# A one-core S4 and PEER mix: the first matmul work is taken from the experts' scores, a row sum is done twice, and a weights' buffer is claimed later

## The chip, the cores and the metric

The kernel runs on one core of a Trainium2 chip. That core has five engines with an instruction stream each: TensorE (PE, matmuls), VectorE (DVE), ScalarE (ACT), GpSimd (POOL) and SyncE (SP), which here issues nearly all DMA transfers. The metric is the device time of one execution in microseconds, and the figure for a kernel is the median of three runs.

## The reference

For 2048 tokens of 576 numbers the program computes two branches and mixes them by a gate:

```
x = A_u                                       # (1, 2048, 576)
g = sigmoid((x * gate_w).sum(-1))
a = S4 convolution of x along the tokens (kernel K from 128 complex poles
    for each of 576 channels, by FFT) + x * Dskip
b: q = x @ w_q                                # 32 heads, two halves of 128
   s1 = q1 . k1, s2 = q2 . k2                 # 64 keys each
   top 2 of s1 and top 2 of s2, 4 sums, top 2 of these -> experts e, softmax g2
   act = gelu(x . u[e])                       # 4096 experts, u, v: (4096, 576)
   b = sum over heads and picks of g2 * act * v[e]
out = g * a + (1 - g) * b
```

## The kernel before

The kernel doesn't gather expert rows. It computes `x . u` for all 4096 experts, places the chosen weights in a dense array of 2048 tokens by 4096 experts, and multiplies that with `v`. Nearly all of TensorE's time is in three products: the scores `s` (tokens by keys, where the keys have been folded into `w_q`), the activations `a` (experts by tokens), and the output `o`. Each is done with operands split into a high and a low fp16 part, three matmuls for one, so each operand is first scaled by a power of two that is found from sums of squares.

Names. `xT` is the tokens, transposed; `xb[tb]` is a block of 512 tokens, scaled and split (`xb[:, 0:4]` high parts, `4:8` low parts, `8` the last 64 of the 576 rows with both). `xs` and `xr` are its raw data in fp32 (512 rows and the last 64). `uhl[c]` with `wrem` is a chunk of 512 experts of `u`, scaled and split in the same way, from raw `us` and `ur`. `whl[c]` with `wrem` is a chunk of four heads of folded weights, built in two halves from raw `wq` (`w_half`): squares on ACT (`wj`), a row sum on PE (`wn`), a fold with the keys on PE (`wb`, 72 small matmuls), and the scaled split on ACT and DVE (`w_tail`). A group `s(c,t)` is 14 matmuls for 128 tokens, followed on DVE by 8 MAX8 and 8 FIND_INDEX8; a group `a(c,tb,j)` is 14 matmuls for 128 experts and 512 tokens, followed by one scaled copy `go` and a store to `g_d`.

What sets the order. The kernel is recorded by cooperating generators under a planner in the kernel's own Python: `clock` is planned PE time, `Engine` objects estimate when each engine is free and each tile is ready, `spawn`, `ready` and `need` suspend a generator until the planned time of its inputs, a PSUM bank or a buffer. The recorded order is final: at run time each engine takes its instructions strictly in that order, and SP its DMA issues. Counted places stand for buffers (`quota`): `slot` 9 large SBUF buffers, `raw` one place (later two) for a raw chunk of `wq` or `us` in work, `sc` four PSUM banks for `s` and `a`.

The head of the program before: SP issues the keys `kt`, the first tokens, the two halves of the first weights, then the first `u`. PE sums the squares of the first tokens (`x`, 5 matmuls), folds both halves of the weights, and then begins with `s(0,0)`. The main loop then takes groups from the lists `groups` (scores) and `acts` (activations) as their inputs come ready. At a change of weights chunk, `w_next` may claim `raw` for the first half of the next chunk once 5 groups of the current chunk are left; the place is given back when that half has been folded, and the fold needs `w_build(c)`, which waits for the last group of the chunk before.

Alongside, from about 100 us to 600 us, the generators of the S4 branch run: `k_front` and `k_gen` (GpSimd, DVE and ACT, with PE's `kP` and `kb`), and `u_stage1`. After that come the transforms, the placing of the picks (`S`), and the output `o`.

Of the kernel before, what the change touches and what calls it, by code (L numbers as in the profile page):

```python
# [13 lines left out]
F16 = mybir.dt.float16  # L14
# [102 lines left out]
class Engine:  # L117


    def __init__(self, eng, ready, clock, key, cost):  # L120
        self.eng, self.ready, self.clock, self.key, self.cost = eng, ready, clock, key, cost
        self.free = 0.0

    def __getattr__(self, op):
        f = getattr(self.eng, op)

        def call(*a, **k):
            out = k.get("out", a[0] if a else None)
            aps = [x for x in (*a, *k.values()) if x is not out and hasattr(x, "tensor")]
            start = max(self.free, self.clock[0], *(self.ready.get(self.key(x), 0.0) for x in aps))  # L130
            self.free = start + self.cost(op, out, a, k)
            self.ready[self.key(out)] = max(self.free + 0.28, self.ready.get(self.key(out), 0.0))
# [5 lines left out]
def body(ctx: ExitStack, tc: tile.TileContext, xT, au, par, logdt, dskip, gatew, wq, kT, uT, vv,  # L138
# [283 lines left out]

    def x_load(tb):
# [3 lines left out]
        dma(a, xT[0:512, c].rearrange("(k p) n -> p k n", p=128))  # L427
        dma(r[0:64], xT[512:576, c])
        dma(r[64:128], xT[512:576, c])
        return a, r  # L430
# [14 lines left out]

    def x_build(tb):
        while tb and tb - 1 not in scaled:
            yield 0.3
        if tb:
# [3 lines left out]
        while tb and 0 not in uhl:  # L453
            yield 0.3
        b = slot([9, 512], F16, f"xb{tb}")
        sq = b[:, 0:5].bitcast(BF16)
        yield from ready(a, r)
        if tb:
            S.activation(sq[:, 0:4, :], a, AF.Square)
        else:  # L460
            S.activation(sq[:, 0:2, :], a[:, 0:2], AF.Square)
            V.tensor_mul(sq[:, 2:4, :], a[:, 2:4], a[:, 2:4])
        S.activation(sq[:, 4, :], r, AF.Square)
        yield from ready(b)
        yield from need("kb")
        p = bank("kb", f"x{tb}")
        for k in range(5):
            mm(p, onesb, sq[:, k, :], k == 0, k == 4)
        yield from ready(p)
        V.tensor_reduce(out=nx[:, tb:tb + 1], in_=p, axis=AX, op=OP.max)  # L470
        free("kb", nx)
        s, i = root_scale(nx[:, tb:tb + 1], 1.02)
        V.tensor_copy(i_x[:, tb:tb + 1], i)
        yield from ready(s)
        for o, i in [(b[:, k], a[:, k, :]) for k in range(4)] + [(b[:, 8], r)]:
            if tb == 0 or S.free > V.free + 2.0:
                V.tensor_scalar(o, i, s, None, op0=OP.mult)
            else:
                S.activation(o, i, AF.Copy, scale=s)
        scaled.append(tb)  # L480
        for k in range(4):
            yield from ready(b)
            V.scalar_tensor_tensor(b[:, 4 + k], a[:, k, :], s, b[:, k], op0=OP.mult, op1=OP.subtract)
# [9 lines left out]
    whl, wl, sk, halves, scaled, squared = {}, {}, [], {}, [], []  # L493
# [23 lines left out]

    def w_half(c, h, w):
        fl = lambda x: x.rearrange("p a b -> p (a b)")
        yield from ready(w)  # L520
        pbs = []
# [1162 lines left out]
```

## Time and profile before

| | us |
|---|---|
| median of 3 runs | 1469.38 |
| lowest and highest | 1467.86, 1471.87 |
| the profiled execution | 1466.58 |
| its span, first to last instruction | 1464.7 |
| PE busy | 1431.2 (98%) |
| DVE busy | 1248.5 (85%) |
| ACT busy | 790.6 (54%) |
| POOL busy | 532.0 (36%) |

The profiled execution is 2.8 us faster than the median of the runs. All waits and durations below are from it. Its span leaves out 1.9 us that lie before the first and after the last instruction.

The page's line numbers are of the kernel before. All work on DVE, ACT and POOL has L133 (the `Engine` helper), all matmuls L213 and all DMA issues L204, so rows are told apart by the names of their tiles. A matmul's duration in a row includes its fill; the rate of a run of matmuls is read from the starts.

### The profile page before, as it was taken

To read this page: it belongs to the slowest core of one execution; us is meant where nothing else is said; L and a number is where in the kernel's file an instruction comes from. 1 tells how busy PE (TensorE), PEld (TensorE's weight loads), DVE (VectorE), ACT (ScalarE), POOL (GpSimd) and SP (SyncE) were. 2 spreads that over 40 slices of the span, in tenths; PEclk is the share of its full clock that TensorE was granted. 3 is DMA by queue.
4 is the path that set the end of the run, shared out by engine and by line. 5 is a ranking of instruction groups with operands and counts; after the bars stand their busy time and mean duration, and the time that the engine had idled before them with its cause. 6 is when DMAs were issued, how large, how long until landed. Compare 5 with 4: busy or idle time off the path is not lost.

```text
span 1464.7 us, 36789 instructions
## 1 busy us (share of the span) xinstructions
PE 1431.2 (98%) x14025; PEld 858.4 (59%) x14028; DVE 1248.5 (85%) x4589; ACT 790.6 (54%) x1315; POOL 532.0 (36%) x511
## 2 busy tenths in 40 slices
PE   5999999999999999999999999998999999999999
PEld 2445454554544544555555444455787787788787
DVE  6989989989999699959899898579998998898860
ACT  5647767698697787434656544576424224223310
POOL 0443545556745645201246799622100110110100
PEclk8999999999999999999999999999999999999999
DMA  9235433372434534384768666677533432442400
GB/s 319 81 93 162 128 94 118 111 213 89 147 104 133 160 107 135 109 263 138 254 211 290 232 200 206 221 239 221 157 111 116 133 125 85 138 147 68 156 10 17
DMA packets 139185, 221.21 MB, mean 151 GB/s; under 512 B 11648, under 2 KB 82688, under 8 KB 132608
## 3 DMA queue, kind: packets, MB, share of 16 engines
q1 hardware_dynamic: 138912, 218.78, 46.5%
q8 instruction: 110, 1.80, 0.5%
q14 instruction: 67, 0.55, 0.1%
q10 hardware_dynamic: 96, 0.07, 0.0%
HBM read 147.51 MB, written 71.30 MB: 149 GB/s over the span
## 4 chain that ended last, share of the span: by engine, by line
PE 84%; DVE 10%; DMA 3%; ACT 1%; issue 1%; SPq 1%; POOL 1%; DVEq 0%; ACTq 0%; POOLq 0%
PE o L213 24%; PE a L213 23%; PE s L213 22%; PE S L213 4%; PE wb L213 2%; PE kb L213 2%; DVE i L133 2%; PE pr L213 2%; DVE m L133 1%; PE u L213 1%; PE y L213 1%; PE kP L213 1%; DVE e L133 1%; PE pv L213 1%; DVE uh L133 1%
## 5 line engine op out<-in xcount | busy, mean ns | idle before, releaser
L213 PE MATMUL o<-vhl,wh 128*128 128x288 f16 x3072 | 387.0, 286 | 0.0
L213 PE MATMUL s<-whl,xb 128*128 128x512 f16 x1536 | 369.5, 382 | 5.0 <-DVE whl L133 4.2
L213 PE MATMUL a<-xb,uhl 128*128 128x512 f16 x1536 | 361.1, 379 | 0.4 <-DVE ko L133 0.4
L213 PEld LDWEIGHTS <-wh 128*128 128x128 f16 x3072 | 296.0, 98 | 76.3 <-issue 3.7
L213 PEld LDWEIGHTS <-xb 128*128 128x128 f16 x1792 | 171.8, 98 | 213.1 <-issue 27.1
L213 PEld LDWEIGHTS <-uhl 128*128 128x128 f16 x1536 | 148.2, 98 | 175.7 <-issue 2.8
L133 DVE FIND_INDEX8 i<-m,s 128x8 uint32<-128x64 f32 x1024 | 206.5, 222 | 0.0
L133 ACT ACTIVATE wh<-gl,s_wg 128x1024 f16<-128x1024 f32 x64 | 68.9, 1137 | 200.3 <-DVE gl L133 200.3
L133 DVE MAX8 m<-s 128x8 f32<-128x64 f32 x1024 | 146.4, 215 | 28.1 <-PE s L213 27.8
L133 POOL TENSOR_TENSOR CS<-CS,ex 128x512 f32<-128x512 f32 x72 | 100.2, 1423 | 139.0 <-DVE ex L133 120.0
L133 POOL TENSOR_TENSOR ya<-ya,db 128x576 f32<-128x576 f32 x16 | 32.0, 2012 | 305.2 <-DMA ya<-in_au_dram 143.6
L133 ACT ACTIVATE go<-a,i_a 128x512 f32<-128x512 f32 x95 | 64.2, 686 | 82.5 <-PE a L213 54.7
L133 POOL TENSOR_TENSOR e<-aN,rt 128x512 f32<-128x512 f32 x72 | 87.5, 1234 | 50.9 <-PE kb L213 47.6
L133 DVE SCALAR_TENSOR_TENSOR wh<-gl,s_wg,wh 128x1024 f16<-128x1024 f32 x64 | 92.4, 1474 | 11.3 <-ACT wh L133 11.3
L133 DVE TENSOR_TENSOR gl<-S,gl 128x256 f32<-128x256 f32 x256 | 90.0, 415 | 7.3 <-PE S L213 7.3
L133 DVE TENSOR_TENSOR Bg<-Be,vals 128x1024 f16<-128x1024 f16 x128 | 90.6, 749 | 2.2
L133 ACT ACTIVATE gl<-gl 128x1024 f32<-128x1024 f32 x64 | 63.5, 1045 | 34.8 <-DMA gl<-g_d 34.8
L133 DVE TENSOR_TENSOR A<-iota_a,vals 128x2048 f16<-128x2048 f16 x64 | 80.5, 1258 | 0.0
L213 PE MATMUL S<-Bg,A 128*128 128x64 f16 x2048 | 73.0, 193 | 5.1 <-DVE Bg L133 4.2
L213 PEld LDWEIGHTS <-A 128*128 128x128 f16 x2048 | 70.6, 97 | 11.2 <-DVE Bg L133 4.1
L213 PE MATMUL s<-wrem,xb 128*128 128x512 f16 x256 | 76.2, 379 | 0.0
L213 PE MATMUL a<-xb,wrem 128*128 128x512 f16 x256 | 76.2, 379 | 0.0
(203 smaller groups left out, 2205.7 us busy)
## 6 DMA issues: line engine op xcount, KB each, us to landing
g_d<-go SPq DMA_DIRECT2D x128, 256.0 KB, 2.7
gl<-g_d SPq DMA_DIRECT2D x32, 1024.0 KB, 5.4
wq<-in_wq_dram SPq DMA_DIRECT2D x16, 1152.0 KB, 6.3
us<-in_au_dram SPq DMA_DIRECT2D x64, 144.0 KB, 3.0
su_d<-us SPq DMA_DIRECT2D x32, 288.0 KB, 2.6
sk_d<-k1o SPq DMA_DIRECT2D x32, 288.0 KB, 2.8
vn<-in_vv_dram SPq DMA_DIRECT2D x32, 288.0 KB, 3.7
ui<-su_d SPq DMA_DIRECT2D x16, 576.0 KB, 4.0
```

Of the source, the lines that this page charges most:

```text
L133: return f(*a, **k)
L213: T.matmul(o, l, r, start=start, stop=stop)
```

## The change

Three things are changed, and the planner's order follows from them in the whole program.

1. The head. SP issues the first tokens (the remainder first, then two halves) and the first `u` in the same way, then the keys, the second block of tokens, the weights and the constants. `x_first` and `scale_first` scale the first tokens by the whole block's sum of squares (taken by ACT's accumulator, summed over partitions by PE in three one-column matmuls) instead of the largest row sum. The first 56 matmuls of PE's main work are `a(0,0,0..3)`, recorded piece by piece: for each part of the tokens and of `u`, four matmuls as soon as it is planned to be there. The folds of the first weights (`fold_first`), their squares and `kn` come later, after the second block of tokens has its scale.
2. `x_norm(0)` computes the row sums of the first tokens twice: 8 matmuls whose result is overwritten while the scale of `u` is not there, and then the 5 that count.
3. `w_next` claims `raw` when 2 groups of the current chunk are left, not 5; the second half of a chunk (`second`) goes ahead of a chunk of `u` that waits for the same place.

Beside these, `Engine.at` lets the planner count a result as ready 0.16 us earlier on the engine that made it, and `x_build` waits for each scaled part by itself.

```diff
+    def halves_load(a, src, c):
+
+        columns.add(a.tensor.name)
+        for m in (0, 2):
+            dma(a[:, m:m + 2], src[128 * m:128 * m + 256, c].rearrange("(k p) n -> p k n", p=128))
...
+    def x_norm(tb, sq):
+
+        yield from need("kb")
+        p = bank("kb", f"x{tb}")
+        if tb == 0:
+            for k in range(8):
+                mm(p, onesb, sq[:, k % 4, :], True, True)
+            while not marks["s"]:
+                yield 0.1
+        for k in range(5):
+            mm(p, onesb, sq[:, k, :], k == 0, k == 4)
+        normed.append(tb)
+        yield from ready(p)
+        while tb == 0 and 1 not in scaled:
+            yield 0.3
+        V.tensor_reduce(out=nx[:, tb:tb + 1], in_=p, axis=AX, op=OP.max)
+        free("kb", nx)
+
+    def x_first():
+
+        a, r = xl.pop(0)
+        b = slot([9, 512], F16, "xb0")
+        first_u[1] = b
+        ahead.append(slot([9, 512], F16, "xb1"))
+        sq = ahead[0][:, 0:5].bitcast(BF16)
+        s, i = yield from scale_first(a, r, sq)
+        spawn(x_norm(0, sq))
+        V.tensor_copy(i_x[:, 0:1], i)
+        for k in range(5):
+            while k == 2 and not marks["s"]:
+                yield 0.1
+            o, lo, src = (b[:, k], b[:, 4 + k], a[:, k, :]) if k < 4 else (b[:, 8], b[64:128, 8], r)
+            p = slice(0, 128) if k < 4 else slice(64, 128)
+            V.tensor_scalar(o, src, s, None, op0=OP.mult)
+            V.scalar_tensor_tensor(lo, src[p], s[p], o[p], op0=OP.mult, op1=OP.subtract)
+            marks["x"].append(V.free + 0.28)
+        scaled.append(0)
+        free("slot", b)
+        xb.append(b)
+
+    def scale_first(a, r, sq, keep=None):
+
+        acc = [newcol() for _ in range(3)]
+        yield from ready(r)
+        S.activation(sq[:, 4], r, AF.Square, accum_out=sc[:, acc[0]])
+        for n, m in enumerate((0, 2)):
+            yield from ready(a[:, m:m + 2])
+            S.activation(sq[:, m:m + 2], a[:, m:m + 2], AF.Square, accum_out=sc[:, acc[n + 1]])
+        yield from ready(sq)
+        yield from need("kb")
+        p = bank("kb", "sq")
+        for n in range(3):
+            mm(p[:, 0:1], onesb, short(acc[n].start, 1), n == 0, n == 2, 0.05)
+        yield from ready(p)
+        out = root_scale(p[:, 0:1], 1.02)
+        if keep is not None:
+            V.tensor_copy(keep, p[:, 0:1])
+        free("kb", out[0])
+        return out
...
+    def fold_first(h, w, pbs):
+        while len(folded) < h or 1 not in scaled:
+            yield 0.2
+        out = []
+        yield from need("kb", 3 + h)
+        yield from w_fold(0, h, w, out, ("kb",) * 3)
+        pbs.extend(out)
+        folded.append(h)
...
+        if c == 0:
+            spawn(fold_first(h, w, pbs))
+        while 1 not in scaled:
+            yield 0.2
...
     def w_next(c, h):
-        while sdone[0] < c - (kdone[0] == NCK) and 8 * NT - len(groups) < NT * c - 5:
+        while sdone[0] < c - (kdone[0] == NCK) and 8 * NT - len(groups) < NT * c - 2:
             yield 0.3
         yield from need("raw")
         take("raw", "raw")
+        if h:
+            second.pop()
...
+        if c == 0:
+            first_u[0] = hl
+            s, i = yield from scale_first(a, r, sq, nu[:, 0:1])
+            marks["s"].append(1)
...
+        if c == 0:
+            for k in range(4):
+                S.activation(hl[:, 0, k, :], a[:, k, :], AF.Copy, scale=s)
+                marks["h"].append(S.free + 0.28)
+            S.activation(rem[:, 0, :], r, AF.Copy, scale=s)
+            marks["h"].append(S.free + 0.28)
         for k in range(4):
-            yield from split(hl[:, 0, k, :], hl[:, 1, k, :], a[:, k, :], s)
-        S.activation(rem[:, 0, :], r, AF.Copy, scale=s)
+            if c:
+                yield from split(hl[:, 0, k, :], hl[:, 1, k, :], a[:, k, :], s)
+                continue
+            while 0 not in scaled:
+                yield 0.1
+            rdy[key(hl)] = marks["h"][k]
+            V.scalar_tensor_tensor(hl[:, 1, k, :], a[:, k, :], s, hl[:, 0, k, :], op0=OP.mult, op1=OP.subtract)
+            marks["u"].append(V.free + 0.28)
...
+    xl = {0: x_load(0)}
+    take("raw", "raw")
+    xl["u"] = u_load(0)
     dma(kt, kT)
-    xl = {0: x_load(0)}
+    xl[1] = x_load(1)
     w_load(0, 0)
     w_load(0, 1)
+    dma(cst, cst_d[:, :KT])
...
+    spawn(x_first())
+    spawn(u_build(0))
+    spawn(w_build(0), 4)
+    spawn(w_half(0, 0, wl[0, 0]), 4)
+    spawn(w_half(0, 1, wl[0, 1]), 4)
+    spawn(k_split(), 4)
+    for tb in range(1, 4):
+        spawn(x_build(tb), 5 * tb)
     spawn(k_params(), 30)
...
+    until(lambda: marks["x"] and marks["h"], 0.1)
+    first = [bank("sc", f"a0_0_{j}") for j in range(4)]
+
+    def landed(kind, k):
+        until(lambda: len(marks[kind]) > k, 0.1)
+        idle(max(0.0, marks[kind][k] - clock[0]))
+
+    for w, n in ((0, 9), (1, 5)):
+        for xk in [x for k in range(4) for x in (k, 4 + k)[:2 - w]] + [8]:
+            k = 4 if xk == 8 else xk % 4
+            landed("x", k)
+            landed("hu"[w], k)
+            for j in range(4):
+                cs = slice(128 * j, 128 * j + 128)
+                mm(first[j], wrems[0][:, w, cs] if k == 4 else first_u[0][:, w, k, cs], first_u[1][:, xk, :],
+                   w == 0 and xk == 0, w == 1 and k == 4)
+            pump()
+    del acts[0:4]
+    if 0 in i_u:
+        V.tensor_scalar(i_a[:, 0, 0:1], i_x[:, 0:1], i_u[0], None, op0=OP.mult)
+    for j in range(4):
+        spawn(act_post(0, 0, j, first[j]))
```

Line numbers in the order below are of each kernel: L133 and L204 before are L140 and L211 now. SP at the head of the program, before:

```order
L204 DMA kt_113<-in_kT_dram 128x128
L204 DMA xs0_119<-in_xT_dram 128x4x512
L204 DMA xr0_120<-in_xT_dram 64x512 x2
L204 DMA wq0_0_124<-in_wq_dram 128x2304
L204 DMA wq0_1_126<-in_wq_dram 128x2304
L204 DMA us0_142<-in_uT_dram 128x4x512
L204 DMA ur0_143<-in_uT_dram 64x512 x2
L204 DMA cst_70<-in_cst_dram 128x576
L204 DMA xs1_210<-in_xT_dram 128x4x512
```

and now:

```order
L211 DMA xr0_119<-in_xT_dram 64x512 x2
L211 DMA xs0_118<-in_xT_dram 128x2x512 x2
L211 DMA ur0_125<-in_uT_dram 64x512 x2
L211 DMA us0_124<-in_uT_dram 128x2x512 x2
L211 DMA kt_113<-in_kT_dram 128x128
L211 DMA xs1_131<-in_xT_dram 128x4x512
L211 DMA xr1_132<-in_xT_dram 64x512 x2
L211 DMA wq0_0_136<-in_wq_dram 128x2304
L211 DMA wq0_1_138<-in_wq_dram 128x2304
L211 DMA cst_70<-in_cst_dram 128x576
```

The first `u` has moved from behind both halves of the weights to a place behind the first tokens, and both are issued in two halves; the keys, which were first, stand behind them.

ScalarE at the head (`xb` and `uhl` with `sc` are squares into the place of the later split, `uhl` with `sci` are the scaled high parts, `vals` is the squares of the keys), before:

```order
L133 ACTIVATE vals_80<-kt_113 128x128
L133 ACTIVATE xb0_136<-xs0_119 128x1024
L133 ACTIVATE xb0_136<-xr0_120 128x512
L133 ACTIVATE wj0_0_163,sc_75<-wq0_0_124 128x1152 x2
L133 ACTIVATE wj0_1_223,sc_75<-wq0_1_126 128x1152 x2
L133 ACTIVATE whl0_135<-wb0_0_2_167,sci_76 128x2x256
L133 ACTIVATE wrem2_116<-wb0_0_4_168,sci_76 64x128 x4
L133 ACTIVATE uhl0_282,sc_75<-us0_142 128x2048
L133 ACTIVATE uhl0_282,sc_75<-ur0_143 128x512
L133 ACTIVATE whl0_135<-wb0_1_0_226,sci_76 128x2x256
L133 ACTIVATE whl0_135<-wb0_1_2_227,sci_76 128x2x256
L133 ACTIVATE wrem2_116<-wb0_1_4_228,sci_76 64x128 x4
```

and now:

```order
L140 ACTIVATE xb1_149,sc_75<-xr0_119 128x512
L140 ACTIVATE xb1_149,sc_75<-xs0_118 128x1024 x2
L140 ACTIVATE uhl0_150,sc_75<-ur0_125 128x512
L140 ACTIVATE uhl0_150,sc_75<-us0_124 128x1024 x2
L140 ACTIVATE uhl0_150<-us0_124,sci_76 128x512 x4
L140 ACTIVATE wrem0_114<-ur0_125,sci_76 128x512
L140 ACTIVATE vals_80<-kt_113 128x128
L140 ACTIVATE xb1_149<-xs1_131 128x2048
L140 ACTIVATE xb1_149<-xr1_132 128x512
L140 ACTIVATE xb1_149<-xs1_131,sci_76 128x512 x4
L140 ACTIVATE wj0_1_279,sc_75<-wq0_1_138 128x1152 x2
L140 ACTIVATE wj0_0_282,sc_75<-wq0_0_136 128x1152 x2
```

The squares of the weights (`wj`) stood ahead of the squares of `u` and the splits of the folded weights ahead of its scaled parts; all of them now stand behind, and the keys' squares and the second block of tokens between.

On PE the head now reads: three matmuls for the scale of the tokens, 8 of `x0`, three for the scale of `u`, 5 of `x0`, then 12 of `a(0,0)`, `kn`, 12 of `a(0,0)`, 5 of `x1`, 16 of `a(0,0)`, the fold `wb0_0`, 12 of `a(0,0)`, `wn0_1`, the last 4 of `a(0,0)`, `wn0_0`, then `a(0,1,0)`, 12 of `a(0,1,1)`, the fold `wb0_1`, the rest of `a(0,1)`, and then `s(0,0)`.

SP at the first change of weights (`wq1_0` and `wq1_1` are the halves of the second chunk, `us_` the loads of `u_stage1`, `go` the activations that are stored), before:

```order
L204 DMA g_d_65<-go0_1_2_720 128x4x128
L204 DMA g_d_65<-go0_1_3_861 128x4x128
L204 DMA wq1_0_923<-in_wq_dram 128x2304
L204 DMA g_d_65<-go0_2_0_1034 128x4x128
L204 DMA g_d_65<-go0_2_1_1056 128x4x128
L204 DMA g_d_65<-go0_2_2_1079 128x4x128
L204 DMA g_d_65<-go0_2_3_1098 128x4x128
L204 DMA us_1112<-in_au_dram 64x576 x2
L204 DMA tu0_1119<-in_tu_dram 128x256
```

and now:

```order
L211 DMA g_d_65<-go0_2_3_1096 128x4x128
L211 DMA su_d_66<-us_934 32x4x576
L211 DMA us_934<-in_au_dram 64x1x576 x2
L211 DMA tu2_1145<-in_tu_dram 128x256
L211 DMA g_d_65<-go0_3_0_1121 128x4x128
L211 DMA su_d_66<-us_934 32x4x576
L211 DMA us_934<-in_au_dram 64x1x576 x2
L211 DMA tu3_1173<-in_tu_dram 128x256
L211 DMA wq1_0_1228<-in_wq_dram 128x2304
L211 DMA su_d_66<-us_934 32x4x576
```

The load of the first half, which went out ahead of the stores of `a(0,2)` and of the first loads of `u_stage1`, now goes out behind `a(0,3,0)` and the first stores of `u_stage1`.

119 lines of the change are left out of this document (67 added, 52 removed).

## The prediction

> **What bounds the kernel now.** I read in this order: the busy time of each engine in long stretches, then PE's waits in the head, then the head row by row. The stretches (us, then PE, PEld, DVE, ACT, POOL busy with the number of instructions, the granted clock, DMA share, GB/s):
>
> ```profile
> 0.00:26.34 26.34, 9.21 (x157) 6.66 (x158) 17.13 (x52) 18.39 (x33) 0.20 (x4) 0.88 0.94 333
> 26.34:66.29 39.95, 39.84 (x175) 17.69 (x177) 36.13 (x143) 21.15 (x33) 15.35 (x10) 0.95 0.31 100
> ...
> 985.25:1025.20 39.95, 35.74 (x341) 22.41 (x340) 39.71 (x53) 25.44 (x33) 11.62 (x8) 1.00 0.74 235
> 1025.20:1065.16 39.96, 38.51 (x472) 30.62 (x470) 39.79 (x63) 17.33 (x19) 5.15 (x3) 1.00 0.52 168
> ...
> 1424.75:1464.70 39.95, 36.36 (x297) 28.81 (x295) 1.98 (x4) 0.00 (x0) 0.00 (x0) 0.99 0.06 16
> sum 1464.70, PE 1431.22 PEld 858.39 DVE 1248.50 ACT 790.61 POOL 532.02; mean PE 38.68 PEld 23.20 DVE 33.74 ACT 21.37 POOL 14.38
> ```
>
> PE is idle for 1464.70 - 1431.22 = 33.5 us. Of these, 26.34 - 9.21 = 17.1 lie in the first 26.34 us. The other 16.4 are spread over 1438 us: 4.2 and 1.4 where DVE is full (39.7 of 40 us), 3.6 at the very end, and some 7 in small pieces. So from 26 us on PE is the bound, with DVE close behind it (36.1 of 40), and what can be had is in the head. PE's waits there, and then its rows there with the rate that follows:
>
> ```profile
> PE x L213 <- ACT xb L133: 4.5, 1, 4.5
> PE s L213 <- DVE whl L133: 4.2, 1, 4.2
> PE sq L213 <- ACT uhl L133: 4.0, 1, 4.0
> PE kn L213 <- ACT vals L133: 3.1, 1, 3.1
> ```
>
> ```profile
> 7.95 2.29 PE L213 MATMUL x<-xb,onesb 128*128 128x512 bf16 x5 [4.54 <-ACT xb L133]
> ...
> 14.35 2.32 PE L213 MATMUL wb<-kt,wq 128*64 128x64 f32 x72
> ...
> 26.34 4.50 PE L213 MATMUL s<-whl,xb 128*128 128x512 f16 x11 [4.20 <-DVE whl L133]
> ...
> 30.67 0.59 PE L213 MATMUL s<-wrem,xb 128*128 128x512 f16 x2
> ...
> 41.24 2.75 PE L213 MATMUL a<-xb,uhl 128*128 128x512 f16 x12
> ...
> 43.84 0.59 PE L213 MATMUL a<-xb,wrem 128*128 128x512 f16 x2
> 44.27 2.75 PE L213 MATMUL a<-xb,uhl 128*128 128x512 f16 x12
> ```
>
> The main work starts at 26.34 and its first 11 matmuls take 30.67 - 26.34 = 4.33 us, 0.39 each; later a whole group of 14 takes 44.27 - 41.24 = 3.03, 0.2165 each. The 11 cost 4.33 - 2.38 = 1.95 us more than they would later. The seconds around it say why (the last three columns are granted clock, DMA share and GB/s):
>
> ```profile
> 20.00:21.00 1.00, 0.16 (x1) 0.10 (x1) 0.98 (x3) 0.97 (x5) 0.00 (x0) 0.55 1.10 267
> ...
> 29.00:30.00 1.00, 1.00 (x4) 0.29 (x2) 0.00 (x0) 0.00 (x0) 0.00 (x0) 0.50 0.65 238
> 30.00:31.00 1.00, 1.00 (x5) 0.44 (x4) 0.00 (x0) 0.00 (x0) 0.00 (x0) 0.83 0.58 158
> ```
>
> The granted clock is 0.50 until shortly after 30 us, that is for the first 4.0 us of unbroken matmuls, after PE had been idle from 16.8 to 20.8.
>
> **The head, step by step.** The durations that the new chain is made of:
>
> ```profile
> 6.84 1.06 ACT L133 ACTIVATE xb<-xs 128x1024 bf16<-128x1024 f32 x1 [3.75 <-DMA xs<-in_xT_dram]
> ...
> 10.79 1.16 ACT L133 ACTIVATE wj<-wq 128x1152 bf16<-128x1152 f32 x1 [2.37 <-DMA wq<-in_wq_dram]
> ...
> 11.71 1.67 DVE L133 TENSOR_SCALAR xb<-xs,sci 128x512 f16<-128x512 f32 x4
> 11.86 0.19 ACT L133 ACTIVATION_READ_ACCUMULATOR wj<-wq 128x1 f32 x1
> ...
> 14.46 0.22 DVE L133 TENSOR_SCALAR sc<-wn,kk 128x1 f32<-128x1 f32 x1 [0.69 <-PE wn L213]
> ...
> 15.15 0.15 DVE L133 COPY invW<-sci 128x1 f32<-128x1 f32 x1
> 15.23 0.74 DVE L133 SCALAR_TENSOR_TENSOR xb<-xs,sci,xb 128x512 f16<-128x512 f32 x1
> ...
> 23.47 2.56 ACT L133 ACTIVATE uhl<-us,sci 128x512 f16<-128x512 f32 x4
> ```
>
> Landing. The first half of the weights lands at 10.8, with 64 + 1024 + 256 + 1152 = 2496 KB issued up to it (issues of the page). Tokens and `u` together are 2560 KB, first in the queue: they land at about 10.95 (64 KB more at some 400 GB/s). The tokens' last half lands at 6.84 + 0.6 = 7.45, since the 256 KB of the remainder now go ahead.
>
> The way by `u`: squares of the last half 1.06 + 0.19, sum on PE with its hand-overs 0.5, scale on DVE 15.15 - 14.46 = 0.69, the first high part 2.56 / 4 = 0.64 and 0.1 for the hand-over: 14.1. The way by PE: squares of the tokens end at 7.45 + 1.25 = 8.7, their sum at 9.0, 8 row sums at 2.29 / 5 = 0.43 (the older row) to 12.4, the sum for `u` to 12.7, 5 more row sums to 13.8 at full clock or 14.9 at half. I take 14.4 for the first `a` matmul; bounds 13.8 and 14.9.
>
> Here the Trainium skill, page "TensorE: Matmul & The Clock Gate", section "What's actually happening", has a rule that speaks against the 8 row sums being enough: the gate is judged over a free-running window of 3413 ns, and so it could open anywhere between one and two windows after work begins. The trace's 4.0 us lie inside that. An estimate from that page: the latest opening would put about 1.0 us on the sum, the earliest would take 0.3 off; no run here shows the phase.
>
> From 14.4 PE does: 8 groups `a(0,0)` and `a(0,1)`, 8 x 3.03 = 24.2; 5 row sums of the second block, 1.1; two folds, 2 x 2.32 = 4.6; `wn` and the small sums, 0.3. Added waits: `kn` now stands behind 12 `a` matmuls, at 17.0, while ACT makes its squares only after five parts of `u`, at about 17.0: 0 to 0.5, I take 0.3, with all of `a` queued behind it. `a(0,1,0)` needs a bank of `a(0,0)`, whose copy waits on DVE for the scale after `wn0_1`; that sum stands 4 matmuls before the end of `a(0,0)`, so of its 0.69 + 0.2 and the copy's 0.7 about 0.9 is left over. So `s(0,0)` starts at 14.4 + 24.2 + 1.1 + 4.6 + 0.3 + 0.3 + 0.9 = 45.8.
>
> Before, the same `a` groups and row sums were still to do at 26.34, with folds and `wn` done: 26.34 + 24.2 + 1.1 + 1.95 for the half clock, less 0.2 for one matmul done at 21.55, is 53.4. Gain in the head: 53.4 - 45.8 = **7.6 us**.
>
> What is costed at nothing. The 8 extra row sums run while `u` is landing; without that cover they would be 3.4. The later weights land at 10.95 + 2496 / 400 = 17.2, and the fold stands at 14.4 + 40 x 0.2165 + 1.1 + 0.3 = 24.5; if they came later, the fold would hold all of PE. The keys and the second tokens land by about 14.4, needed from 16.7. On DVE three parts of the tokens (1.67 / 4 = 0.42 and 0.74 each) and five low parts of `u` (0.74) are left when the scale of `u` is there at 13.5, so they end at about 20.7; the low parts of `u` are needed after 36 matmuls, at 23.6; that slack of 2.9 us is the cover. The planner's 0.16 us moves no engine's own time.
>
> **The weights' raw place.** The first half now goes out up to 3 groups (9.1 us) later, the second sooner after the first. How long a second half takes is seen at the first change, from the fold of the first half to the row sum of the second:
>
> ```profile
> 118.85 2.32 PE L213 MATMUL wb<-kt,wq 128*64 128x64 f32 x72
> ...
> 124.09 0.38 SPq L204 DMA_DIRECT2D wq<-in_wq_dram  x1
> ...
> 129.82 1.16 ACT L133 ACTIVATE wj<-wq 128x1152 bf16<-128x1152 f32 x1 [0.65 <-DMA wq<-in_wq_dram]
> ...
> 132.18 0.19 ACT L133 ACTIVATION_READ_ACCUMULATOR wj<-wq 128x1 f32 x1
> ...
> 132.64 0.19 PE L213 MATMUL wn<-sc,onesb 128*128 128x1 bf16 x2
> ```
>
> The squares are done 132.4 - 118.85 = 13.5 us after the fold began, 0.3 before PE came to `wn`. In the new order 37 `a` matmuls, the fold and small ones stand between, some 12.2 us: a wait of 0 to 1.3, of which I take 0.7. From the last score of a chunk to the first of the next the new order holds 36, 85, 98 and 18 us of PE's work at the first four changes (34, 91, 59 and 23 before), and at the last three scores run on without a gap, as before. There is other work ahead of the late half everywhere, so I add nothing more. It can't gain either: before, no PE wait on `wb` after the head is in the list.
>
> **Sum.** 7.6 - 0.7 = 6.9 off. The profiled execution took 1466.6 and would take 1459.7; the median of the runs is 2.8 above that execution, so 1469.4 - 6.9 = **1462.5**. It holds only if the shift is carried through; after the head PE is the bound, and where DVE is (985 to 1065) its work is the same and begins earlier too.
>
> **Rivals.** A change within 0.3%, 4.4 us, can't be told from none here.
> 1. The head gains little: `u` comes late. For it: us to landing (queue view, first 40 us) of two loads of `u`:
>
> ```profile
> us<-in_uT_dram SPq DMA_DIRECT2D x2, 1024.0 KB, 13.4
> ```
> Issued by 4.5 and 13.4 later is 17.9, 7 us after my 10.95, and the gain would be 0.6: 1468.8. Against it: that load stood behind 2.3 MB of weights. With cold row sums and DVE late in the splits, a part of it is enough to come under 4.4. Chance 0.16, no change.
> 2. Slower: the late claim starves PE at the changes of weights. From issue to the end of the squares a half takes 132.4 - 124.1 = 8.3 us, and the lead of two groups is 6.1. If PE had nothing else, 2.2 us of each half would be bare, 14 halves, 31 us: 1493. It outweighs the head from 11.3 / 14 = 0.8 us a half. Against it stand the 18 to 98 us of other work. If half of it comes through, 1478. Chance 0.16.
> 3. The new order also loses less in the small pieces, at most some 7 us: 1455.5. Chance 0.06.
>
> **Numbers.** The forecast has 0.62, with 1458 to 1465 as its own range. Faster by over 0.3% is it and rival 3, 0.68; same is rival 1, 0.16; slower rival 2, 0.16. The range of 1455 to 1472 leaves out most of rival 2.
>
> **What would show it.** Right: the first `a` matmul between 13.8 and 14.9 at under 0.25 us each; the first `s` at 45 to 47; PE idle in the head under 12 us and after it still about 16. Wrong: a first `a` after 17; PE waiting on DVE `xb` or `uhl` inside `a(0,0)`; PE waits on `wq`, `wj` or `whl` after 100 us that add up to more than 3 us; or PE idle growing in the stretches from 100 to 600.

## The result: the head gains what was predicted, and the rest of the program loses more

The changed kernel takes 1481.7 us, median of five runs (1479.8 to 1483.5); the kernel before, on the same chip, 1468.2 (1466.1 to 1471.9). The ratio is 1.0088 with a 95% interval of 1.0070 to 1.0106: slower by 0.9%, where 0.5% faster was predicted. The profiled execution spans 1479.4 us, the one of before 1464.7.

The stretches of the changed kernel (us, then PE, PEld, DVE, ACT, POOL busy with the number of instructions, the granted clock, DMA share, GB/s):

```profile
0.00:26.34 26.34, 17.28 (x121) 8.41 (x123) 16.65 (x46) 16.89 (x28) 0.20 (x4) 1.00 0.92 317
26.34:66.29 39.95, 38.99 (x264) 19.04 (x261) 29.15 (x95) 18.94 (x31) 12.34 (x9) 1.00 0.42 137
60.00:600.00 540.00, 523.78 (x4878) 261.73 (x4877) 494.18 (x1846) 383.75 (x566) 286.87 (x226) 0.99 0.40 121
600.00:980.00 380.00, 373.92 (x3312) 189.15 (x3311) 321.40 (x1991) 194.59 (x500) 197.66 (x258) 1.00 0.66 224
```

The later two stretches of the kernel before:

```profile
60.00:600.00 540.00, 537.13 (x4964) 269.98 (x4964) 487.08 (x1826) 392.38 (x574) 287.90 (x227) 1.00 0.42 126
600.00:980.00 380.00, 376.37 (x3388) 191.19 (x3386) 313.75 (x1955) 202.92 (x512) 188.06 (x249) 1.00 0.66 220
```

In the head PE is now idle for 26.34 - 17.28 = 9.1 us instead of 17.1; 3.6 us of the 17.28 are the 8 added row sums, so idle time alone overstates the gain. From 60 to 600 us it is idle for 16.2 us instead of 2.9, and from 600 to 980 for 6.1 instead of 3.6. So the gain of the head is there, and it is lost again behind it, with more. Over the whole span PE is idle for 1479.4 - 1439.0 = 40.4 us instead of 33.5, which is 6.9 of the 14.7 us by which the span grew; the other 7.8 are busy time of PE, of which the added row sums are 3.6. What PE waited for from 60 to 600 us, in the changed kernel (us in total, times, longest):

```profile
PE u L220 <- DVE uh L140: 8.6, 11, 2.3
PE kP L220 <- DVE CS L140: 1.8, 1, 1.8
PE kb L220 <- issue: 1.4, 1, 1.4
```

and in the kernel before:

```profile
PE kb L213 <- issue: 1.0, 1, 1.0
PE u L213 <- DVE uh L133: 0.7, 2, 0.5
```

More than half of the new waits stand at one place, the matmuls `u` of `u_stage1`, which in PE's fixed order wait for the low part `uh` that VectorE makes. These waits also cost clock. Two of them, and the microseconds behind them:

```profile
118.39 0.41 PE L220 MATMUL u<-uh,tu 128*128 128x288 f16 x2 [1.60 <-DVE uh L140]
118.63 0.81 PE L220 MATMUL a<-xb,uhl 128*128 128x512 f16 x3
119.81 0.72 PE L220 MATMUL u<-uh,tu 128*128 128x288 f16 x4 [0.37 <-DVE uh L140]
```

```profile
119.00:120.00 1.00, 0.63 (x5) 0.26 (x3) 0.97 (x3) 0.24 (x1) 1.00 (x2) 1.00 0.08 16
120.00:121.00 1.00, 1.00 (x6) 0.53 (x5) 0.97 (x9) 0.75 (x3) 1.00 (x2) 0.63 0.00 0
121.00:122.00 1.00, 1.00 (x4) 0.45 (x3) 1.00 (x11) 0.55 (x1) 1.00 (x2) 0.50 0.00 0
...
124.00:125.00 1.00, 1.00 (x7) 0.51 (x6) 1.00 (x11) 0.02 (x1) 0.00 (x0) 1.00 0.63 215
```

PE waits 1.60 and then 0.37 us, and then runs for 3.4 us at a granted clock of 0.50, which is another 1.7 us lost. The trace has two more such stretches of 3.4 us, with waits of 2.26 us at 485 and 3.42 us at 714; the kernel before has one between 60 and 980 us, at 890.

### The profile page after: what moved, and what is told of

It is laid out like the page before. It is cut to its first block, busy times and chain, and to the rows that moved or that the text cites. A ratio compares the mean times of both kernels' runs of the same rounds, so it can differ in the third digit from the quotient of the medians.

```text
span 1479.4 us, 36839 instructions
## 1 busy us (share of the span) xinstructions
PE 1439.0 (97%) x14041; PEld 859.8 (58%) x14041; DVE 1258.4 (85%) x4613; ACT 768.6 (52%) x1285; POOL 533.9 (36%) x516
## 4 chain that ended last, share of the span: by engine, by line
PE 72%; DVE 19%; issue 2%; ACT 2%; POOL 2%; DMA 1%; SPq 0%; DVEq 0%; ACTq 0%; POOLq 0%
PE o L220 24%; PE a L220 17%; PE s L220 17%; PE S L220 4%; DVE i L140 4%; PE wb L220 2%; DVE m L140 2%; PE kb L220 2%; DVE Y L140 2%; DVE uh L140 2%; DVE e L140 2%; PE pr L220 1%; PE y L220 1%; PE k L220 1%; POOL vf L140 1%
## 5 line engine op out<-in xcount | busy, mean ns | idle before, releaser
L220 PE MATMUL a<-xb,uhl 128*128 128x512 f16 x1536 | 364.8, 381 | 1.6 <-ACT go L140 1.6
L220 PE MATMUL s<-whl,xb 128*128 128x512 f16 x1536 | 365.8, 380 | 0.0
L140 DVE FIND_INDEX8 i<-m,s 128x8 uint32<-128x64 f32 x1024 | 206.8, 224 | 0.0
L140 ACT ACTIVATE wh<-gl,s_wg 128x1024 f16<-128x1024 f32 x63 | 67.6, 1137 | 210.3 <-DVE gl L140 210.3
L140 POOL TENSOR_TENSOR ya<-ya,db 128x576 f32<-128x576 f32 x16 | 30.2, 1899 | 346.9 <-DMA ya<-in_au_dram 240.7
L140 DVE MAX8 m<-s 128x8 f32<-128x64 f32 x1024 | 146.2, 216 | 9.0 <-PE s L220 8.1
L140 POOL TENSOR_TENSOR CS<-CS,ex 128x512 f32<-128x512 f32 x72 | 97.6, 1387 | 149.2 <-DVE ex L140 140.9
L140 DVE SCALAR_TENSOR_TENSOR wh<-gl,s_wg,wh 128x1024 f16<-128x1024 f32 x64 | 93.3, 1486 | 13.1 <-ACT wh L140 13.1
L140 DVE TENSOR_TENSOR gl<-S,gl 128x256 f32<-128x256 f32 x256 | 89.8, 416 | 8.5 <-PE S L220 4.9
L140 POOL TENSOR_TENSOR e<-aN,rt 128x512 f32<-128x512 f32 x72 | 85.8, 1211 | 26.5 <-PE kb L220 26.3
L140 ACT ACTIVATE go<-a,i_a 128x512 f32<-128x512 f32 x81 | 54.9, 684 | 74.9 <-PE a L220 47.0
L140 DVE TENSOR_TENSOR Bg<-Be,vals 128x1024 f16<-128x1024 f16 x128 | 85.9, 713 | 2.2
L140 ACT ACTIVATE gl<-gl 128x1024 f32<-128x1024 f32 x64 | 63.6, 1045 | 40.7 <-DMA gl<-g_d 40.7
L140 DVE TENSOR_TENSOR A<-iota_a,vals 128x2048 f16<-128x2048 f16 x64 | 78.7, 1230 | 0.0
```

Of the source, the lines that this page charges most:

```text
L140: return f(*a, **k)
L220: T.matmul(o, l, r, start=start, stop=stop)
```

## The experiments

Four theories were on record at first. A: the planner's allowance of 0.16 us (`Engine.at`) gives VectorE work earlier than the chip does it. B: the later claim of the weights' raw place is the loss. C: the new head leaves VectorE empty, and later it is the bound. D: any change of the planner's numbers makes a new order of the whole program, and a new order falls out by chance. E and F came later. All times stand against runs of the kernel before on the same chip, whose median was 1466.5 to 1468.2 us in these comparisons.

**The parts, one at a time.** The allowance is taken out of the changed kernel:

```
-        return t - 0.16 if self.own.get(n) == t else t
+        return t
```

> The changed kernel without the planner's 0.16 us allowance for results on the same engine; nothing else is edited. Theory A (the allowance makes the planner believe that VectorE is freer than it is, so it gives it more copies and PE waits behind them): the head's gain of some 7 us is kept, 1460 to 1466, copies of a on VectorE about 42 of 128 and PE waits after the head under 20 us. Theory B (the weights' place that is claimed later): still about 1480. Theory C (the head leaves VectorE empty, which is then the bound): still about 1480. Theory D (any new order falls out by chance, some 10 us either way): somewhere between 1460 and 1485, without a pattern over the runs.

It took 1484.1 us, ratio 1.0107 (1.0090 to 1.0124). It isn't faster, and A's 1460 to 1466 is missed. It has one large wait of PE, and the rows ahead of it tell what it waited for:

```profile
377.79 0.39 ACT L140 ACTIVATE us<-u 128x288 f32<-128x288 f32 x1
378.21 0.58 SPq L211 DMA_DIRECT2D su_d<-us  x1
...
378.85 1.24 SPq L211 DMA_DIRECT2D us<-in_au_dram  x2
...
382.56 0.78 ACT L140 ACTIVATE uh<-us,sci 128x576 f16<-128x576 f32 x1 [4.38 <-DMA us<-in_au_dram]
...
383.32 1.21 DVE L140 TENSOR_TENSOR Y<-e,CS 128x1024 f32<-128x1024 f32 x1
...
386.11 1.91 DVE L140 SCALAR_TENSOR_TENSOR uh<-us,sci,uh 64x576 f16<-64x576 f32 x1
...
388.07 0.64 PE L220 MATMUL u<-uh,tu 128*128 128x288 f16 x2 [11.72 <-DVE uh L140]
```

This is the loop of `u_stage1`: ScalarE copies a result, SP stores it, SP loads the next tokens into the same buffer, ScalarE makes the high part, VectorE the low part, and only then PE goes on. VectorE had the products of `k_gen`, from 383.32 to 386.1, ahead of the low part. All this time PE had nothing else in its order. Most of this wait is in the plan: by the planner's clock PE has nothing to do for some 9 us ahead of the `s` group that this `u` stands in. The chip does that group's first six matmuls at once and idles before `u` instead.

The allowance is put into the kernel before, alone (the methods `at` and `own` of the change, nothing else):

> The kernel before with the planner's 0.16 us allowance alone. Theory A: slower, 1475 to 1485, with 54 of 128 copies of a on VectorE and PE waits on VectorE between 60 and 600 us of 10 or more. Theories B and C: as before, 1465 to 1471. Theory D: anywhere within 10 us.

1499.1 us, ratio 1.0213 (1.0188 to 1.0237). Alone it costs 31 us, which is the most of any part and more than any of the theories had. So A has the sign right where the allowance is added, and not where it is taken away; it doesn't add up with the rest.

The rule of the raw place is put into the kernel before, alone:

```
-        while sdone[0] < c - (kdone[0] == NCK) and 8 * NT - len(groups) < NT * c - 5:
+        while sdone[0] < c - (kdone[0] == NCK) and 8 * NT - len(groups) < NT * c - 2:
```

> The kernel before with the weights' raw place claimed 2 groups ahead instead of 5, alone. Theory B: slower, 1475 to 1485, with PE waits at the changes of weights. Theories A and C: as before, 1465 to 1471. Theory D: anywhere within 10 us.

1470.0 us, ratio 1.0017 (1.0007 to 1.0026). The opposite in the changed kernel, the old number and no right of way for the second half (the wait on `second` in `u_build` removed):

> The changed kernel with the raw place claimed 5 groups ahead again, and without the second half's right to go first. Theory B: the head's gain is kept, 1460 to 1466. Theories A and C: still about 1480. Theory D: somewhere between 1460 and 1485.

1494.1 us, ratio 1.0174 (1.0157 to 1.0191): 12 us slower than the changed kernel, and its longest wait of `u<-uh,tu` for `uh` is 15.9 us, at a place where the plan itself leaves PE without work for some 12 us. B is out: the rule costs 0.2% in the one kernel, and taking it back made the other 12 us slower. That a part has no fixed price speaks for D.

**How far a new order alone goes.** One price of the planner is changed by 0.001 us, in the kernel before and in the changed one, so that nothing differs but small decisions:

```
-        t = 0.085 + 0.00083 * size(out)
+        t = 0.086 + 0.00083 * size(out)
```

> The kernel before, with the planner's fixed price of a ScalarE instruction at 0.086 us instead of 0.085: the same work, a plan that differs in small places. Theory D (any new order falls out by chance, some 10 us either way, and the old one was a lucky one): 1475 to 1495. Theories C and E (the loss has a place: VectorE full from 66 to 510 us, or TensorE's matmuls u of the sequence transform that stand in its fixed order behind VectorE's low parts uh): nothing is moved there that matters, 1466 to 1472, and the waits of TensorE from 60 to 600 us stay under 5 us.

> The changed kernel with the same tiny step of the planner's price. Theory D: anything from 1470 to 1500. Theory C: the plan now gives VectorE 52 of the copies go instead of 47, five more of 0.7 us, so 1483 to 1487. Theory E: the sum of the u waits decides, near the changed kernel's own, 1477 to 1487.

The kernel before goes from 1466.5 to 1478.1, ratio 1.0074 (1.0051 to 1.0097). The changed kernel comes to 1477.8, ratio to the kernel before 1.0074 (1.0048 to 1.0101). A step that means nothing costs the old kernel nearly as much as the change did. It isn't lost in the same place: from 60 to 600 us PE waits no more than before, the `u` waits of this run are still short, and its largest wait behind the head is in the key transform,

```profile
704.27 0.64 PE L213 MATMUL k<-ksb,tk 128*128 128x288 f16 x2 [4.45 <-ACT k1o L133]
```

so theories C and E, which both expected no loss here, failed with it.

**The place of the waits.** Theory E: the loss is the wait of `u` for `uh`. In the changed kernel PE's matmuls `u` are planned 1.5 us later:

```
-                yield from ready(h)
+                yield from ready(h, late=1.5)
```

> The changed kernel with one edit in the sequence transform: TensorE's matmuls u are planned 1.5 us after VectorE's low part uh is planned to be ready, not at once. Theory E: the 11 waits u<-uh,tu of 60 to 600 us (8.6 us together) and the two half-clock windows of 3.4 us that follow them (1.7 us each) go: 1481.7 - 8.6 - 3.4 = 1469.7, 1468 to 1474. Theory C (VectorE is simply full there): the waits move to other matmuls, and the time stays at 1478 to 1485. Theory D: 1470 to 1500.

1476.5 us, ratio 1.0063 (1.0040 to 1.0086). That is 5.2 us less than the changed kernel, where E expected 8 to 14 less (1468 to 1474). The waits of `u` go from 8.6 us to 1.3, as E says, but PE's waits turn up elsewhere:

```profile
PE kP L220 <- DVE ko L140: 2.3, 3, 1.8
PE a L220 <- DVE i L140: 2.3, 1, 2.3
PE a L220 <- issue: 2.0, 1, 2.0
PE u L220 <- DVE uh L140: 1.3, 2, 1.1
```

Theory C says that VectorE has too much to do. It does have more of the copies `go` than before (the views of the tile `go` of the kernel before, then of the changed one: how often, then the shortest, middle and longest in ns):

```profile
L133 DVE TENSOR_SCALAR go<-a,i_a x33: 734/750/752, 47.9 to 998.2; 128x512 f32<-128x512 f32 x33
```

```profile
L140 DVE TENSOR_SCALAR go<-a,i_a x47: 731/744/753, 30.9 to 1016.2; 128x512 f32<-128x512 f32 x47
```

So 15 of them were given back to ScalarE by the planner's threshold:

```
-        if S.free <= V.free + 0.5:
+        if S.free <= V.free + 1.5:
```

> The changed kernel with one number in the choice of the engine for the copies go: VectorE takes one only where ScalarE's planned end is more than 1.5 us past its own, not 0.5. VectorE then has 32 of them as in the kernel before (33), not 47: 15 copies of about 0.7 us, 10 us less. Theory C: VectorE is the bound from 66 to 510 us, so most of it comes back: 1471 to 1475. Theory E: VectorE's low parts come earlier too, but ScalarE, which makes the high parts ahead of them, is later: 1474 to 1482. Theory D: 1470 to 1500.

1489.1 us, ratio 1.0146 (1.0118 to 1.0175): slower still, and its waits of `u` for `uh` are 12.4 us. C, in this form, is out: less work for VectorE didn't help, in an order that was new again as a whole.

**What tells a good order from a bad one.** The planner has its own clock, `clock[0]`, which counts what it expects PE to do. Where it stands at the last matmul, when the program is written out, is called the end of the plan here; it is no time of the chip. Theory F takes the time apart into this end and what the chip falls behind it. In the runs so far that was 11 to 18 us where the plan has no allowance and 25 to 38 where it has; F forecasts the same for new plans. It was then tried on four plans whose ends lie far apart. Two are one number away from the changed kernel without the allowance:

```
-                yield from ready(h)
+                yield from ready(h, late=0.5)
```

> The changed kernel without the planner's 0.16 us allowance, and with TensorE's matmuls u planned 0.5 us after VectorE's uh instead of at once. Theory F (the time is where the planner's own clock ends, and on top of it what the chip falls behind the plan: in the runs so far 11 to 18 us where the plan has no allowance, 25 to 38 where it has): this plan of all ends latest, at 1497.8 on its own clock, against 1473.1 without the 0.5 us, so 1509 to 1516. Theory E (the matmuls u wait for VectorE on the chip, and margin there helps): 1484 or less. Theory D (chance on the chip, the plan says nothing): 1470 to 1500.

```
-    spawn(k_params(), 30)
+    spawn(k_params(), 20)
```

> The changed kernel without the allowance, and with the first step of the kernel generation put in at 20 us of the plan instead of 30, where VectorE is empty. Theory F: the plan ends at 1456.2, so 1467 to 1474, faster than the changed kernel by some 10 us. Theory D: 1470 to 1500. Theory C (VectorE's empty head is the loss): work moves into it, 1470 to 1478.

They took 1508.2 us, ratio 1.0286 (1.0262 to 1.0310), and 1466.0, ratio 0.9992 (0.9981 to 1.0003). The two programs do the same work and differ in two numbers of the planner; 42.2 us were measured between them, where the ends of their plans are 41.6 apart. Each lies about 1 us below the range of F. D, with chance on the chip (1470 to 1500), is out, and so is E as the whole cause, since more margin at `u` was to help (1484 or less). In the slow one PE's loss is where the plan has it, at the end of the `s` groups:

```profile
980.00:1100.00 120.00, 80.37 (x902) 57.39 (x900) 107.69 (x159) 63.95 (x80) 29.27 (x17) 0.83 0.58 196
```

```profile
PE S L220 <- DVE Bg L140: 25.5, 13, 9.7
PE y L220 <- DMA tf<-in_tf_dram: 9.9, 1, 9.9
```

The other two have several of the planner's numbers changed. They were picked, out of some 540 plans, because they end early; the second has half the allowance, 0.08 us:

> The changed kernel's head and weights' rule with other numbers of the planner (no allowance; a ScalarE instruction 0.086 us; u 3 us after uh; the second half of the sequence transform 4 us after the first; copies go to VectorE from 1.2 us on; the later blocks of tokens 4 us apart; kernel generation put in at 24 us; a lag of 2.5 us allowed). Theory F: of some 540 plans with other numbers the one without allowance that ends first, at 1449.7, 6.1 us before the old kernel's plan (1455.8): 1461 to 1468, faster than the old kernel by 0 to 7 us. Theory D: 1470 to 1500. Theory E: the matmuls u have 3 us of margin, but the old kernel had none and lost nothing there: 1466 to 1476.

> As the run with other numbers of the planner, but with half the allowance, 0.08 us, and the plan that then ends first of all, at 1447.1. Theory F: the chip falls behind it by a value between the two kinds, 16 to 26 us: 1463 to 1473, so in spite of the shorter plan no faster than the plan without allowance. Theory D: 1470 to 1500. Theory A (the allowance itself is harmless): 1447 + 11 to 18, 1458 to 1465.

1467.9 us, ratio 1.0011 (0.9999 to 1.0023), and 1463.3, ratio 0.9977 (0.9964 to 0.9989). Both lie at the edge of what F gave (1461 to 1468 and 1463 to 1473), but F had the second no faster than the first. The second is faster than both kernels, by 0.2% of the old one. PE's stretch from 60 to 600 us is nearly as full there as in the old kernel, behind the new head:

```profile
0.00:26.34 26.34, 17.50 (x133) 8.63 (x135) 16.91 (x47) 17.22 (x29) 0.20 (x4) 1.00 0.94 326
60.00:600.00 540.00, 535.68 (x5068) 269.90 (x5067) 484.91 (x1886) 396.61 (x588) 289.48 (x232) 0.99 0.42 128
```

**Whose allowance it is.** In the kernel before, the allowance is given to VectorE alone, and to ScalarE alone (`give` is 0.16 for that engine and 0 for the others):

```
+        return t - self.give if self.own.get(n) == t else t
...
+    V.give = 0.16
```

> The kernel before with the 0.16 us allowance for results that VectorE reads of itself, and not for ScalarE. The plan ends at 1457.5 on its own clock (1455.8 without it). Theory F with VectorE at fault (it is the fullest engine after TensorE, and its planned lead over the chip is the margin): the chip falls 25 to 38 us behind, 1483 to 1495. With ScalarE at fault: 1468 to 1475.

> The kernel before with the allowance for ScalarE alone. The plan ends at 1457.9. With VectorE at fault: 11 to 18 us behind, 1469 to 1476. With ScalarE at fault: 1483 to 1495. If each has a share, both runs lie at 1472 to 1485.

The two plans end within 0.4 us of each other. VectorE's took 1487.7 us, ratio 1.0143 (1.0126 to 1.0160); ScalarE's 1472.5, ratio 1.0033 (1.0022 to 1.0045). Each lies where F with VectorE at fault had it (1483 to 1495 and 1469 to 1476). So of these two it is VectorE's; GpSimd, which has the allowance too in the changed kernel, wasn't tried alone. With VectorE's, PE's stretch looks as in the changed kernel, with the same wait on top, though the head is the old one:

```profile
60.00:600.00 540.00, 520.88 (x4744) 258.33 (x4743) 511.36 (x1909) 362.67 (x535) 289.82 (x223) 1.00 0.39 118
```

```profile
PE u L221 <- DVE uh L140: 5.5, 5, 2.2
PE a L221 <- DVE i L140: 2.3, 2, 1.4
```

**The head alone.** The changed kernel without the allowance, with the old number for the raw place and without `second`:

> The new head alone: the changed kernel without the allowance, with the old rule for the weights' raw place and without the second half's right of way. The plan ends at 1462.8, of which 13 us are idle time that the plan itself holds from 500 to 600 us. Theory F: 1473 to 1480, slower than the kernel before although the first scores of the first block start 7 us sooner. What was predicted of the head (7.6 us off, the rest as before): 1459 to 1462.

1463.5 us, ratio 0.9974 (0.9965 to 0.9984), faster than before by 3.4 us; F expected 10 us more, and missed. In 60 to 600 us PE is idle for 540 - 532.39 = 7.6 us in all, while this plan leaves PE without work for some 12 us between 577 and 603 of its own clock: what the plan idles needn't be lost on the chip.

```profile
60.00:600.00 540.00, 532.39 (x4937) 267.37 (x4936) 493.02 (x1800) 387.92 (x569) 285.21 (x227) 1.00 0.41 124
```

All kernels by these two numbers (end of the plan; measured median; the difference, which is how far the chip falls behind; the kernel before lies 11 to 12 behind, by which of its medians is taken):

```
kernel                            end      measured  behind
no allowance for VectorE
  before                          1455.8   1466.9    11.1
  raw place's rule alone          1457.9   1470.0    12.1
  before, 0.086                   1460.0   1478.1    18.1
  ScalarE's allowance alone       1457.9   1472.5    14.6
  changed, no allowance           1473.1   1484.1    11.0
    and u 0.5 us later            1497.8   1508.2    10.4
    and generation at 20 us       1456.2   1466.0     9.8
    and other numbers             1449.7   1467.9    18.2
  head alone                      1462.8   1463.5     0.7
half the allowance, other numbers 1447.1   1463.3    16.2
allowance for VectorE
  changed                         1448.2   1481.7    33.5
  changed, 0.086                  1452.9   1477.8    24.9
  changed, u 1.5 us later         1447.7   1476.5    28.8
  changed, copies to ScalarE      1451.6   1489.1    37.5
  changed, old raw rule           1468.0   1494.1    26.1
  allowance alone                 1470.1   1499.1    29.0
  VectorE's allowance alone       1457.5   1487.7    30.2
```

Without VectorE's allowance the chip falls 1 to 18 us behind the plan, with it 25 to 38; the two sets don't meet. Half of it, with 16.2, lies among those without. "Behind" is only the measured time less the end of the plan, so it splits the loss and doesn't explain it. The changed kernel's plan ends 1455.8 - 1448.2 = 7.6 us before the old one. That this is the very gain that was predicted is chance: the head alone has a plan that ends 7.0 us later than the old one, and the changed kernel's own plan without the allowance ends at 1473.1. The chip then falls 33.5 behind it, not 11 to 12, and the sum of -7.6 and about 22 is the measured 14.

**Where the chip falls behind.** The planner's start of each VectorE instruction (`start` in `Engine`) can be set beside its start in the trace. By how many us the chip is late, the median of the instructions that are planned in four stretches of 100 us:

```
planned from (us)            100    400    700   1000
before                      -0.5    0.1   -0.4    4.8
ScalarE's allowance alone    0.9   -2.6    2.4    7.9
head alone                  -4.0   -3.7  -10.2   -4.2
VectorE's allowance alone    3.7   12.9   19.9   24.9
allowance alone              4.7    8.8   15.3   21.7
changed                      1.6    9.7   19.8   27.0
```

With VectorE's allowance the chip is not late at one place; it becomes later through most of the program. The same comparison says what is wrong with the prices. The planner takes a result to be ready 0.28 us after the instruction's end, and with the allowance 0.12. The lower number is about right for the pair that it was made for:

```profile
13.22 0.16 DVE L140 TENSOR_SCALAR sc<-sq 128x1 f32<-128x1 f32 x1 [0.69 <-PE sq L220]
13.41 0.15 DVE L140 TENSOR_SCALAR sci<-sc 128x1 int32<-128x1 int32 x1
```

The second reads the first's result and starts 0.19 us after it; the planner takes 0.066 + 0.12 = 0.186 with the allowance and 0.346 without. Over the 445 neighbours on VectorE for which the changed kernel's plan counts these 0.12 us, the chip takes 0.092 in the mean, from the planned end of the first to the start of the second, and 0.086 over the 436 of the kernel before, which are planned at 0.28. But where the plan puts one VectorE instruction right behind another, the chip takes longer than planned, with waits for other engines counted in: 84 us over 2941 neighbours in the changed kernel, 101 over 2975 before. A clean piece of it is the four low parts of `u` in the head (17.46 to 20.12, shown below): 0.665 us each, where the planner takes 0.60. So in the kernel before, 436 x (0.28 - 0.086) = 84 us that were charged too much stood against 101 charged too little; in the changed kernel it is 445 x (0.12 - 0.092) = 12 against 84. The old price was too high, and the excess was the slack that the other prices needed. This is worked out from the traces; no run has the allowance with the other prices corrected.

What stays open: how much of the lateness each of these prices makes, since VectorE isn't the bound all the time; and why removing the allowance alone gave so late a plan (1473.1). Also open is whether the 0.7 of the head alone is anything but a lucky order: it keeps ahead of its plan from the start, and gains most at 600 us, where the plan leaves PE without work.

## Why the prediction was wrong

The head came out as worked out, to 0.2 us at its end. PE's rows of the changed kernel there:

```profile
9.20 3.57 PE L220 MATMUL x<-xb,onesb 128*128 128x512 bf16 x8
...
14.80 2.75 PE L220 MATMUL a<-xb,uhl 128*128 128x512 f16 x12
17.39 0.22 PE L220 MATMUL kn<-vals,onesb 128*128 128x128 bf16 x1
...
31.58 2.75 PE L220 MATMUL a<-xb,uhl 128*128 128x512 f16 x12 [0.96 <-ACT go L140]
...
46.02 1.24 PE L220 MATMUL s<-whl,xb 128*128 128x512 f16 x5
```

- The first `a` matmul: 14.4 was taken, with bounds of 13.8 and 14.9; it is 14.80, with the row sums at 3.57 / 8 = 0.45 us each, the older rate (0.43), which was taken for the 8; the 5 behind them took from 13.04 to 14.80, 0.35 each, between the two rates that made the bounds. Then 12 `a` matmuls take 17.39 - 14.80 = 2.59 us, 0.216 each.
- `kn`: 0.3 was allowed, and there is no wait. The bank of `a(0,1,0)`: 0.9 was taken, 0.96 measured. `s(0,0)`: 45.8 was taken, 46.02 measured. The gain of the head by the same working is 53.4 - 46.0 = 7.4 us instead of 7.6.
- Landing: `u` was to be there at 10.95, and ScalarE's squares of its last half start at 11.82, after a wait of 0.25 for the load, 0.9 later. The row sums on PE hid nearly all of it: PE waits 0.21 us for these squares, and the first `a` has no wait of its own.

```profile
11.82 1.06 ACT L140 ACTIVATE uhl<-us 128x1024 bf16<-128x1024 f32 x1 [0.25 <-DMA us<-in_uT_dram]
```

- The low parts of `u` on VectorE were to end at about 20.7. They end at 20.12 + 0.73 = 20.85, and PE doesn't wait for them:

```profile
17.46 2.74 DVE L140 SCALAR_TENSOR_TENSOR uhl<-us,sci,uhl 128x512 f16<-128x512 f32 x4
...
20.12 0.73 DVE L140 SCALAR_TENSOR_TENSOR wrem<-ur,sci,wrem 64x512 f16<-64x512 f32 x1
```

- The raw place: 0.7 was taken at the first change. The load of the second half goes out at 129.58, its squares end 7.9 us later, and the row sum finds them done:

```profile
129.58 0.34 SPq L211 DMA_DIRECT2D wq<-in_wq_dram  x1
...
137.33 0.19 ACT L140 ACTIVATION_READ_ACCUMULATOR wj<-wq 128x1 f32 x1
...
139.41 0.19 PE L220 MATMUL wn<-sc,onesb 128*128 128x1 bf16 x2
```

It costs nothing there, so this term was 0.7 too high; the rule alone, with the new order that it makes, costs 0.2% (the run on the kernel before). The slower rival, which hung on this place, had the right sign for a reason that didn't come about: no wait of PE on `wq`, `wj` or `whl` is among those of 60 to 600 us.

The step that failed is in the part on what is costed at nothing: "The planner's 0.16 us moves no engine's own time." That is true of an instruction's length and beside the point, since the planner's prices set the order of the whole program. Alone this edit costs 31 us (2.1%), and given to VectorE alone 21 (1.4%), while the other two parts alone give -0.3% and +0.2%. In the changed kernel the chip falls 33.5 us behind the plan instead of 11 to 12. Taking the edit out again doesn't bring the forecast by itself (1484.1), since that plan ends 25 us later; other plans without it, behind the same head, took 1466.0 and 1467.9. The sentence behind the sum failed with it: the result "holds only if the shift is carried through; after the head PE is the bound, and where DVE is (985 to 1065) its work is the same". The plan carried the shift through and the chip did not. VectorE's work wasn't the same either, with 47 of the copies instead of 33, and that PE is full from 60 to 600 us is a property of the order and not of the work: three other orders without the allowance keep it (with 0.086, with the raw rule alone, with generation at 20 us PE idles 1.7 to 3.3 us there), others don't, and the planner's step of 0.001 us takes 0.7% from the old kernel elsewhere.

The prediction named the sign that came true, "PE idle growing in the stretches from 100 to 600", but gave no rival a price for it. A rival "the new order keeps PE less full" was to be had from the trace: VectorE, busy for 36 of 40 us where PE is full (487 of 540 from 60 to 600 us), leaves little for a plan to be wrong by.

With the head alone the forecast of 1462.5 would have met the measured 1463.5, but by luck in part: the gain is half of what was forecast (3.4 us instead of 6.9), from a lower time of the kernel before (1466.9 instead of 1469.4).

## What to carry to other kernels

Where a planner writes the order, a change of one of its prices is a change of the whole program: before a result is put down to the edit, build the same kernel with a price moved by a thousandth and see how far that goes (here 0.7%). A price that is too high may be the slack that the other prices need; lowering it alone to what one pair of instructions takes made a shorter plan and a slower kernel here. Parts of such a change are told apart by running each alone, and their prices don't add up: head, raw rule and allowance alone gave 0.9974, 1.0017 and 1.0213, together 1.0088.

## What was not expected of the hardware

How long the clock stays at half after a wait isn't fixed. After 1.60 and 0.37 us of waiting it was 3.4 us, shown above. After the wait of 11.72 us in the run without the allowance:

```profile
387.00:388.00 1.00, 0.00 (x0) 0.00 (x0) 1.00 (x1) 0.00 (x0) 1.00 (x2) 0.50 0.00 0
388.00:390.00 2.00, 1.93 (x6) 0.86 (x6) 1.97 (x14) 1.23 (x2) 2.00 (x2) 0.50 0.00 0
390.00:392.00 2.00, 2.00 (x7) 0.79 (x6) 2.00 (x14) 1.97 (x3) 1.58 (x2) 0.50 0.00 0
392.00:394.00 2.00, 2.00 (x7) 0.78 (x6) 1.94 (x10) 2.00 (x4) 0.00 (x0) 0.57 0.20 46
394.00:396.00 2.00, 2.00 (x27) 0.87 (x29) 1.84 (x18) 1.97 (x3) 0.00 (x0) 1.00 0.27 85
```

PE works again from 388.07, and the clock is full only from 393.7 (0.57 over the two us up to 394 is 0.50 with the last 0.3 us at full), so 5.6 us of work ran at half: 2.8 us lost on top of the 11.72. The stretch at half began at 380.1, while PE was idle, and lasted 13.7 us, four times the 3.4 of the short ones. After the wait of 15.95 us in the run with the old raw rule it was 5.5 us of work, from 336.13 to 341.7.

The Trainium skill, page "TensorE: Matmul & The Clock Gate", section "Why this matters for your kernels", asks for no gap of PE over some 3 us between bursts. This trace doesn't bear that out as a safe bound: two gaps of 1.60 and 0.37 us with 1.05 us of matmuls between them (118.39 to 119.44) were enough to bring the half clock. The same page's section "What's actually happening" gives a window of 3413 ns; the 3.4 us at half agree with it.
